# Splitting the transposed rows ahead of the evacuation, and the product g behind both, in a fused convolution and feed-forward kernel on one core

## The chip, the cores and the metric

The kernel runs on one NeuronCore of a Trainium2 chip. The core has five engines that matter here: TensorE (PE, with its weight loads shown apart as PEld), VectorE (DVE), ScalarE (ACT), GpSimd (POOL) and SyncE (SP, which issues the DMAs). Each engine works through its own queue in order; engines wait for each other through semaphores. The metric is the device time of one execution in microseconds, as the median of several runs. Lower is better.

## What is computed

The first stage is a convolution along the sequence whose seven taps differ for every position and head: the taps are a softmax of `weight_gen`. The second stage is a feed-forward layer with the activation h cos h. Sizes: 8 x 4096 tokens, 192 channels, 8 heads of 24 channels, 7 taps, 2048 hidden columns; x and the taps arrive in float32, the two weight matrices in float64.

```python
w = exp(weight_gen - max(weight_gen, axis=-1))
w = w / (sum(w, axis=-1) + 1e-9)                      # [B, S, H, 7]
x_pad = concatenate([zeros(B, 6, D), x], axis=1)
x_unf = x_pad[:, arange(S)[:, None] + arange(7)[None, :], :].reshape(B, S, 7, H, 24)
y = einsum('bshk,bskhg->bshg', w, x_unf).reshape(B * S, D)
h = y @ w_in                                          # [32768, 2048]
g = h * cos(h)
out = (g @ w_out).astype(float32)                     # [32768, 192]
```

## The kernel before

**Tiling.** Each of the 128 partitions holds a run of 256 consecutive tokens. A block is four tokens of every partition (R = 4), so 512 tokens; there are 64 blocks (NB). The 2048 hidden columns are taken in pairs of chunks of 128, eight pairs a block (NPAIR). One period of the main loop (L537) is one pair of one block; there are 512 periods (N) and a tail of six (LAG). Products are made accurate by splitting an operand into a high part, rounded for PE, and a low rest, with three products in place of one: x_hi and x_lo for the mixed rows, ghi and glo for g, wa_hi, wa_lo, wb_hi and wb_lo for `w_in`.

**Mixing.** `attention` (L213) computes the seven products and six sums of a block on POOL. `attentions` (L457) is a generator, and every period takes some steps of it (L585), so that this work lies between the other work of POOL. A block's mixing may start when the block two before it is transposed (L459), because its buffer `xa` exists twice. `until_mixed` (L468) puts the remaining steps into the queue at once.

**Transposing.** PE needs the mixed rows with channels on partitions. For the first blocks (up to WHOLE) `transpose_all` (L276) transposes a whole block into a PSUM tile of the kind that also holds h, in pair 5 of the block before. Later blocks are transposed row by row: `transpose_row` (L285) puts a row's transposed channels into columns 384 to 511 of the accumulator tile `acc`, whose columns 0 to 383 hold sums of the output. `split` (L268) then reads the transposed rows twice: ACT writes x_hi (L270), DVE writes x_lo (L272), which needs x_hi. The x_hi and x_lo tiles exist twice, by turns for even and odd blocks.

**The feed-forward period.** For period i, PE computes h of pair i in two portions: `ffn_in_first` (L318, matmuls L326) before and `ffn_in_second` (L332, matmuls L343) after `ffn_out` (L380), which multiplies g of six periods ago (j = i - 6) with `w_out` into `acc` (L400). The elementwise work on h of pair i - 1 is a chain between ACT and DVE: turn (L353, ACT: h plus a quarter, rounded to an integer), fraction (L357, DVE), cos (L361, ACT) and g (L364, DVE). For pair i - 2, ACT makes ghi (hi, L370) and DVE glo (lo, L374). h has three PSUM tiles; the one that pair i takes is free when lo of pair i - 3 is done.

**The accumulator.** `acc` (L387) is one PSUM tile of two banks, and there is only one (the pool at L79). Two periods fill it, an even j and an odd j: a group. After the odd one, `evacuate` (L412) reads it: ACT copies the sums into a `part` tile (L421; here called the evacuation), then `split` reads the transposed rows. The first matmul of the next group can only overwrite `acc` when these reads are over. POOL adds the parts (L437, L438), and SP stores four rows of a block at a time (L443), three periods later.

**What sets the order.** The order in which the text issues instructions is the order in each engine's queue; the last loop (L590) nails it down with a dependency between neighbours. In a period the text issues: turn of i - 1, hi of i - 2, fraction and cos of i - 1, lo of i - 2, g of i - 1 (L539 to L552), then PE's matmuls (L561 to L568), then the evacuation and the split (L576), then a step of the softmax (L584), then mixing steps. Which row of which block lies in which accumulator is fixed in `ffn_out` (L406) and again in `evacuate` (L422):

```python
bt = group // R + 2
if WHOLE < bt < NB:
    transpose_row(bt, group % R, acc, s)
```

The softmax of the next sixteen rows is started in every fourth block and runs one step a period (L580 to L584); its exponential (L183) is ACT's, and needs another function table than the cosine.

Of the kernel before, what the change touches and what calls it, by code (L numbers as in the profile page):

```python
# [11 lines left out]
F32 = mybir.dt.float32  # L12
# [8 lines left out]
P = 128  # L21
# [20 lines left out]
def tile_softmax_conv_then_cos_ffn(  # L42
# [17 lines left out]
    R = 4  # L60
# [7 lines left out]
    HALF = NPAIR // 2  # L68
    LAG = 6
    TR = 5  # L70
    WHOLE = 6
    TMP = 6
    CW = 512

    const = ctx.enter_context(tc.tile_pool(name="const", bufs=1))
# [209 lines left out]
    def transpose_row(b, r, acc, s):  # L285

        xa = mixed[b]
        for q in range(2):
            rs = slice(q * D2, (q + 1) * D2)
            nc.tensor.matmul(acc[:, q ^ s, 2 * D + q * D2:2 * D + (q + 1) * D2],  # L290
                             lhsT=xa[rs, r, columns(q ^ s)], rhs=ident[rs, rs], is_transpose=True,
                             start=False, stop=True, skip_group_check=True)
        if r == R - 1 and s == 1:
            transposed.add(b)
# [23 lines left out]
    def ffn_in_first(i):  # L318

        b, pair = divmod(i, NPAIR)  # L320
        x_hi, x_lo = xT[b]
        h = ps_h.tile([P, 2, CT], F32, name="h")
        for m, (w, v) in enumerate(((wa_hi, x_lo), (wa_lo, x_hi), (wa_hi, x_hi))):
            for q in range(2):
                rs = slice(q * D2, (q + 1) * D2)
                nc.tensor.matmul(  # L326
                    h[:, q, :], lhsT=w[rs, chunk(pair, q)], rhs=v[rs, 0, :],
                    start=(m == 0), stop=False, skip_group_check=True)
        hs[i] = h
        traded(h)  # L330
# [49 lines left out]
    def ffn_out(j):  # L380

        b, m = divmod(j, 2 * R)
        half, m = divmod(m, R)
        tp, s = divmod(m, 2)
        group = j // 2
        if s == 0:
            accs[group] = ps_m.tile([P, 2, CT], F32, name="acc")  # L387
        acc = accs[group]
        whole = j + LAG >= N
        for lo in range(2):  # L390
            for c in range(2 * HALF):
                pair, n = divmod(c, 2)
                g = g_parts[b * NPAIR + half * HALF + pair][lo]
                fc = half * 2 * HALF + c
                for q in range(1 if whole else 2):
                    rs = slice(0, P) if whole else slice(q * D2, (q + 1) * D2)
                    bank = q ^ s
                    t = 2 * tp + bank
                    to, w = (acc[:, bank, 0:2 * D], wo) if lo == 0 else (acc[:, bank, 0:D], wo_b)
                    nc.tensor.matmul(  # L400
                        to, lhsT=g[rs, n, t * P:(t + 1) * P], rhs=w[rs, fc, :],
                        start=(lo == 0 and c == 0 and (whole or s == 0)),
                        stop=(lo == 1 and c == 2 * HALF - 1 and (whole or s == 1)),
                        skip_group_check=True)
            if lo == 0:
                bt = group // R + 2  # L406
                if WHOLE < bt < NB:
                    transpose_row(bt, group % R, acc, s)
        if s == 0 and not whole:
            traded(acc)  # L410

    def evacuate(j):  # L412
        b, m = divmod(j, 2 * R)
        half, m = divmod(m, R)
        tp, s = divmod(m, 2)
        if s == 0:
            return
        group = j // 2
        acc = accs.pop(group)
        part = work.tile([P, 2, 2 * D], F32, name=f"part{half}", bufs=2)  # L420
        nc.scalar.activation(out=part, in_=acc[:, :, 0:2 * D], func=AF.Copy, scale=TWO_PI)  # L421
        bt = group // R + 2  # L422
        if WHOLE < bt < NB:
            r = group % R
            yield from split(bt, acc[:, :, 2 * D:], slice(r * P, (r + 1) * P))
        if half == 0:
            sums[(b, tp)] = part
            return
        if tp == 0:
            fin_t = work.tile([P, R, D], F32, name="fin")  # L430
            finals[b] = fin_t
        fin = finals[b]
        old = sums.pop((b, tp))
        last = b == NB - 1
        eng = nc.vector if last else nc.gpsimd
        ts = slice(2 * tp, 2 * tp + 2)
        eng.tensor_tensor(out=part, in0=part, in1=old, op=ALU.add)  # L437
        eng.tensor_tensor(out=fin[:, ts, :], in0=part[:, :, 0:D], in1=part[:, :, D:2 * D],  # L438
                          op=ALU.add)
        if tp == 1 or last:  # L440
            t0 = 2 * tp if last else 0
            def store(t0=t0):
                nc.sync.dma_start(out=o_v[:, :, (b * R + t0) * D:(b * R + 2 * tp + 2) * D],  # L443
                                  in_=fin[:, t0:2 * tp + 2, :].rearrange("p r d -> p (r d)"))

            if last:
                store()
            else:
                stores[j + LATE] = store
        if tp == 1:  # L450
            finals.pop(b)
            for pair in range(NPAIR):
                g_parts.pop(b * NPAIR + pair)
# [83 lines left out]
    for i in range(N + LAG + 1):  # L537

        if 0 <= i - 1 < N:  # L539
            act_turns(i - 1)  # L540
        if 0 <= i - 2 < N:
            act_hi(i - 2)
        for c in converts.get(i - 1, ()):
            next(c)
        if 0 <= i - 1 < N:
            dve_fraction(i - 1)
            act_cos(i - 1)
        all_of(*converts.pop(i - 1, ()))
        if 0 <= i - 2 < N:
            dve_lo(i - 2)  # L550
        if 0 <= i - 1 < N:
            dve_g(i - 1)  # L552
        if i == N + LAG:
            break
        b, pair = divmod(i, NPAIR)
        j = i - LAG
        if b < NB and pair == 0:
            assert b in transposed
        if 0 <= j and j % (2 * R) == 0 and WHOLE < j // (2 * R) + 2 < NB:
            until_mixed(j // (2 * R) + 2)  # L560
        if j < 0:  # L561
            ffn_in_whole(i)
        else:
            if i < N:
                ffn_in_first(i)
            ffn_out(j)
            if i < N:
                ffn_in_second(i)  # L568
        tr = ()
        if pair == TR and b + 1 <= WHOLE:  # L570
            until_mixed(b + 1)
            tr = (transpose_all(b + 1),)
        if j in stores:
            stores.pop(j)()
        if j >= 0:
            all_of(evacuate(j), *tr)  # L576
        else:
            all_of(*tr)
        load_weights(i + AHEAD)
        if b % SB == SB - 1 and pair == SMP and b + 4 < NB:  # L580
            r0 = (b + 4) * R
            sm = softmax(r0, min(r0 + RW, RPP), nc.gpsimd)
        if i >= NPAIR + SMP:
            next(sm, None)  # L584
        for _ in range(4 if i == 0 else 2 + i % 2 if i < 60 else 2):  # L585
            next(bg, None)


# [39 lines left out]
```

## Time and profile before

| | us |
|---|---|
| median of 3 runs | 2451.38 |
| lowest and highest of these | 2450.24 and 2451.68 |
| the profiled execution's own time | 2449.39 |
| its span, first to last instruction | 2447.6 |

| engine | busy us | of the span |
|---|---|---|
| PE | 2278.4 | 93% |
| DVE | 2034.2 | 83% |
| POOL | 1848.4 | 76% |
| ACT | 1833.8 | 75% |

The granted PE clock has a mean of 0.985 over the span. The page lists groups of instructions by source line, with the number of instructions, their busy time, the mean duration in nanoseconds and the idle time of their engine just before them. Each of the six instructions of the elementwise chain runs 512 times: turn 1024 ns, hi 1012 and cos 1060 on ACT; fraction 1222, g 1232 and lo 1214 on DVE. The evacuation runs 256 times with 794 ns. The timeline gives single instructions with start and duration in microseconds, merged where neighbours are alike ("x16"), and, in brackets, the idle time of the engine before them and what ended it. An instruction on DVE or ACT may show its start a little before its predecessor's end, since the engines pipeline.

### The profile page before, as it was taken

Reading aid. Unit: us, or ns where it says so; the run is one execution under the profiler, and the core shown is the slowest. Engines: PE = TensorE matmul, PEld = TensorE weight load, DVE = VectorE, ACT = ScalarE, POOL = GpSimd, SP = SyncE. Lnnn points to the kernel's source line nnn. Section 1 sums busy time; section 2 is a strip of 40 time slices with the busy share of each in tenths; the row PEclk is TensorE's granted clock in tenths of the full one; section 3 lists DMA queues with packets and bytes.
Section 4 is the critical chain, followed back from the end, with each engine's and each line's share of the span. In section 5 each row is a group of like instructions: output and inputs, shape, how many; then the busy total and the mean of one; then the engine's idle time right before and its main releaser. Section 6 shows DMA issues by size and latency. Waiting matters only on the chain.

```text
span 2447.6 us, 60709 instructions
## 1 busy us (share of the span) xinstructions
PE 2278.4 (93%) x26436; PEld 1951.2 (80%) x26436; DVE 2034.2 (83%) x1923; ACT 1833.8 (75%) x2117; POOL 1848.4 (76%) x1206
## 2 busy tenths in 40 slices
PE   2799999999999999999999999999999999999998
PEld 1577887878788788888878788788888878788887
DVE  8878788888888888888888888888888888888886
ACT  3667777777777777777777777777777777777776
POOL 7589777878878878777878878878777778878730
PEclk8799999999999999999999999999999999999999
DMA  5112111111112112111111112112111111211100
GB/s 145 36 40 54 43 35 47 46 32 47 48 31 54 41 29 54 46 32 47 47 31 46 48 31 54 43 28 54 43 35 47 47 32 47 49 29 48 25 14 21
DMA packets 25689, 105.56 MB, mean 43 GB/s; under 512 B 2654, under 2 KB 6486, under 8 KB 25422
## 3 DMA queue, kind: packets, MB, share of 16 engines
q1 hardware_dynamic: 25422, 101.67, 16.9%
q8 instruction: 207, 3.39, 0.6%
q14 instruction: 60, 0.49, 0.1%
HBM read 76.50 MB, written 25.17 MB: 42 GB/s over the span
## 4 chain that ended last, share of the span: by engine, by line
PE 53%; DVE 25%; ACT 12%; issue 9%; DMA 1%; ACTq 0%; SPq 0%; DVEq 0%
PE acc L400 30%; PE h L343 19%; DVE turn L357 9%; DVE glo L374 8%; ACT turn L353 7%; DVE x_lo L272 4%; PE h L326 4%; DVE h L364 1%; ACT x_hi L270 1%; ACT L183 1%; ACT turn L361 1%; ACT ghi L370 1%; PE acc L290 1%; DVE den L187 1%; DMA taps<-in_weight_gen_dram 1%
## 5 line engine op out<-in xcount | busy, mean ns | idle before, releaser
L357 DVE TENSOR_TENSOR turn<-h,turn 128x1024 f32<-128x1024 f32 x512 | 625.7, 1222 | 365.6 <-ACT turn L353 365.5
L400 PE MATMUL acc<-wo,ghi 64*128 64x384 f32 x8144 | 838.5, 343 | 50.1 <-DVE x_lo L272 47.2
L400 PEld LDWEIGHTS acc<-wo,ghi 64*128 64x128 f32 x8144 | 723.6, 187 | 173.4 <-DVE x_lo L272 145.9
L353 ACT ACTIVATE turn<-h 128x1024 int32<-128x1024 f32 x512 | 524.4, 1024 | 298.6 <-PE h L343 296.1
L244 POOL TENSOR_TENSOR xa<-xa,pr 128x768 f32<-128x768 f32 (+1 forms) x384 | 705.4, 1837 | 5.0
L361 ACT ACTIVATE turn<-turn 128x1024 f32<-128x1024 f32 x512 | 542.8, 1060 | 221.5 <-DVE turn L357 221.2
L364 DVE TENSOR_TENSOR h<-h,turn 128x1024 f32<-128x1024 f32 x512 | 631.0, 1232 | 13.8 <-ACT turn L361 13.8
L374 DVE TENSOR_TENSOR glo<-h,ghi 128x1024 bf16<-128x1024 f32 x512 | 621.8, 1214 | 1.1 <-ACT ghi L370 1.1
L224 POOL TENSOR_TENSOR pr<-xt,taps 128x768 f32<-128x768 f32 (+1 forms) x384 | 586.9, 1536 | 18.3
L437 POOL TENSOR_TENSOR part<-part,part 128x768 f32<-128x768 f32 x126 | 232.2, 1843 | 483.4 <-ACT part L421 483.3
L370 ACT CAST ghi<-h 128x1024 fp32r<-128x1024 f32 x512 | 518.0, 1012 | 8.4 <-DVE h L364 8.2
L400 PE MATMUL acc<-wo_b,glo 64*128 64x192 bf16 x8144 | 424.3, 243 | 0.0
L400 PEld LDWEIGHTS <-glo 64*128 64x128 bf16 x8144 | 331.4, 94 | 25.4 <-issue 7.8
L326 PE MATMUL h<-x_lo,wa_hi 64*128 64x512 f32 x1012 | 206.4, 402 | 56.9 <-DVE glo L374 42.6
L343 PE MATMUL h<-x_lo,wa_hi 64*128 64x512 f32 x1012 | 241.9, 473 | 0.0
L421 ACT ACTIVATE part<-acc 128x768 f32<-128x768 f32 x256 | 203.3, 794 | 9.2 <-PE acc L400 9.2
L343 PE MATMUL h<-x_lo,wb_hi 64*128 64x512 f32 x1012 | 202.4, 395 | 0.0
L326 PE MATMUL h<-x_hi,wa_hi 64*128 64x512 f32 x1012 | 201.6, 393 | 0.0
L343 PE MATMUL h<-x_hi,wa_hi 64*128 64x512 f32 x1012 | 201.1, 392 | 0.0
L326 PE MATMUL h<-x_hi,wa_lo 64*128 64x512 f32 x1012 | 200.7, 391 | 0.0
L343 PE MATMUL h<-x_hi,wb_hi 64*128 64x512 f32 x1012 | 200.1, 390 | 0.0
L343 PE MATMUL h<-x_hi,wb_lo 64*128 64x512 f32 x1012 | 199.5, 389 | 0.0
(74 smaller groups left out, 2047.7 us busy)
## 6 DMA issues: line engine op xcount, KB each, us to landing
xt<-in_x_dram SPq DMA_DIRECT2D x62, 960.0 KB, 6.8
out_dram<-fin SPq DMA_DIRECT2D x63, 384.0 KB, 3.4
taps<-in_weight_gen_dram SPq DMA_DIRECT2D x15, 448.0 KB, 4.3
raw<-in_moe_w_out_dram SPq DMA_DIRECT2D x8, 384.0 KB, 5.3
raw<-in_moe_w_in_dram SPq DMA_DIRECT2D x6, 256.0 KB, 6.1
raw<-in_moe_w_in_dram SPq DMA_DIRECT2D x3, 512.0 KB, 12.2
xt<-in_x_dram SPq DMA_DIRECT2D x1, 768.0 KB, 12.0
xt<-in_x_dram SPq DMA_DIRECT2D x1, 540.0 KB, 6.7
```

The lines of the kernel that those rows point to most:

```text
L224: eng.tensor_tensor(out=dst.rearrange("p r (h g) -> p r h g", h=H), in0=xt[:, k + ra:k + rb, :].rearrange("p r (h g) -> p r h g", h=H), in ...
L244: eng.tensor_tensor(out=xa[:, ra:rb, 0:D], in0=xa[:, ra:rb, 0:D], in1=old[:, ra:rb], op=ALU.add)
L326: nc.tensor.matmul(h[:, q, :], lhsT=w[rs, chunk(pair, q)], rhs=v[rs, 0, :], start=(m == 0), stop=False, skip_group_check=True)
L343: nc.tensor.matmul(h[:, 1 - q, :], lhsT=w[rs, cs], rhs=v[rs, part, :], start=False, stop=(m == len(prods) - 1), skip_group_check=True)
L353: nc.scalar.activation(out=t.bitcast(I32), in_=hs[i], func=AF.Identity, bias=0.25, scale=1.0)
L357: nc.vector.tensor_tensor(out=t, in0=hs[i], in1=t.bitcast(I32), op=ALU.subtract)
L361: nc.scalar.activation(out=t, in_=t, func=AF.Sin, bias=SIN_BIAS, scale=SIN_SCALE)
L364: nc.vector.tensor_tensor(out=hs[i], in0=hs[i], in1=turns.pop(i), op=ALU.mult)
L370: nc.scalar.copy(out=hi, in_=hs[i])
L374: nc.vector.tensor_tensor(out=lo, in0=hs.pop(i), in1=hi.bitcast(F32), op=ALU.subtract)
L400: nc.tensor.matmul(to, lhsT=g[rs, n, t * P:(t + 1) * P], rhs=w[rs, fc, :], start=(lo == 0 and c == 0 and (whole or s == 0)), stop=(lo == 1 ...
L437: eng.tensor_tensor(out=part, in0=part, in1=old, op=ALU.add)
```

## The change

Four things change together.

- In `evacuate` the split comes before the evacuation: ACT's queue has x_hi and then the copy into `part`; x_lo follows x_hi on DVE. In the main loop g of i - 1 is issued behind the evacuation and the split, not ahead of PE's matmuls; the split of a whole block (`tr`) comes behind g.
- The rows of a block are transposed one group, that is two periods, later: row r of block bt lies in group 4 bt + r - 7, before in 4 bt + r - 8. The last row is then split in the last period before the block's first. `until_mixed` moves along. In `ffn_in_first` the product with x_lo comes last, before it came first.
- WHOLE is 5, before 6: block 6 is transposed by rows.
- TMP, the number of `turn` buffers, is 5, before 6; `part0` has three buffers, before two; fewer mixing steps are issued in the first 48 periods (three in every fourth period and two in the others, before two and three by turns).

```diff
@@ -68,8 +68,8 @@
-    WHOLE = 6
-    TMP = 6
+    WHOLE = 5
+    TMP = 5
@@ -320,7 +320,7 @@
-        for m, (w, v) in enumerate(((wa_hi, x_lo), (wa_lo, x_hi), (wa_hi, x_hi))):
+        for m, (w, v) in enumerate(((wa_lo, x_hi), (wa_hi, x_hi), (wa_hi, x_lo))):
@@ -403,9 +403,9 @@
             if lo == 0:
-                bt = group // R + 2
+                bt, r = divmod(group + 2 * R - 1, R)
                 if WHOLE < bt < NB:
-                    transpose_row(bt, group % R, acc, s)
+                    transpose_row(bt, r, acc, s)
@@ -417,12 +417,11 @@
         acc = accs.pop(group)
-        part = work.tile([P, 2, 2 * D], F32, name=f"part{half}", bufs=2)
+        bt, r = divmod(group + 2 * R - 1, R)
+        if WHOLE < bt < NB:
+            yield from split(bt, acc[:, :, 2 * D:], slice(r * P, (r + 1) * P))
+        part = work.tile([P, 2, 2 * D], F32, name=f"part{half}", bufs=(3 if half == 0 else 2))
         nc.scalar.activation(out=part, in_=acc[:, :, 0:2 * D], func=AF.Copy, scale=TWO_PI)
-        bt = group // R + 2
-        if WHOLE < bt < NB:
-            r = group % R
-            yield from split(bt, acc[:, :, 2 * D:], slice(r * P, (r + 1) * P))
@@ -548,16 +547,15 @@
-        if 0 <= i - 1 < N:
-            dve_g(i - 1)
...
-        if 0 <= j and j % (2 * R) == 0 and WHOLE < j // (2 * R) + 2 < NB:
-            until_mixed(j // (2 * R) + 2)
+        bt, r = divmod(j // 2 + 2 * R - 1, R)
+        if 0 <= j and j % 2 == 0 and r == 0 and WHOLE < bt < NB:
+            until_mixed(bt)
@@ -573,16 +571,17 @@
         if j >= 0:
-            all_of(evacuate(j), *tr)
-        else:
-            all_of(*tr)
+            all_of(evacuate(j))
+        if 0 <= i - 1 < N:
+            dve_g(i - 1)
+        all_of(*tr)
...
-        for _ in range(4 if i == 0 else 2 + i % 2 if i < 60 else 2):
+        for _ in range(4 if i == 0 else 3 if i < 48 and i % 4 == 0 else 2):
             next(bg, None)
```

## The prediction

> **What bounds the kernel now.** I read the page's busy shares and its chain first, then the list of waits, then the timeline of one steady stretch, row by row.
>
> ```profile
> PE 2278.4 (93%) x26436; PEld 1951.2 (80%) x26436; DVE 2034.2 (83%) x1923; ACT 1833.8 (75%) x2117; POOL 1848.4 (76%) x1206
> ...
> PE 53%; DVE 25%; ACT 12%; issue 9%; DMA 1%; ACTq 0%; SPq 0%; DVEq 0%
> ```
>
> ```profile
> POOL part L437 <- ACT part L421: 483.3, 122, 23.9
> ...
> PEld acc L400 <- DVE x_lo L272: 145.9, 228, 0.9
> ```
>
> PE is the busiest engine, yet DVE and ACT hold 37% of the chain, so PE does not run free. Where it stops is plain: 228 times, once for each group whose accumulator also carries transposed rows, the first weight load of the next group waits for x_lo (L272). POOL has 483 us of waiting for the evacuation and is not on the path.
>
> The timeline of two periods (the first evacuates, the second does not), engine by engine; columns are start, duration, engine, line:
>
> ```profile
> 1202.95 1.03 ACT L353 ACTIVATE turn<-h 128x1024 int32<-128x1024 f32 x1 [1.30 <-PE h L343]
> 1203.87 1.01 ACT L370 CAST ghi<-h 128x1024 fp32r<-128x1024 f32 x1
> 1205.27 1.06 ACT L361 ACTIVATE turn<-turn 128x1024 f32<-128x1024 f32 x1 [0.39 <-DVE turn L357]
> 1206.23 0.80 ACT L421 ACTIVATE part<-acc 128x768 f32<-128x768 f32 x1
> 1206.92 0.37 ACT L270 ACTIVATE x_hi<-acc 128x256 fp32r<-128x256 f32 x1
> 1207.19 1.02 ACT L353 ACTIVATE turn<-h 128x1024 int32<-128x1024 f32 x1
> ...
> 1204.01 1.22 DVE L357 TENSOR_TENSOR turn<-h,turn 128x1024 f32<-128x1024 f32 x1 [1.09 <-ACT turn L353]
> 1205.15 1.21 DVE L374 TENSOR_TENSOR glo<-h,ghi 128x1024 bf16<-128x1024 f32 x1
> 1206.36 1.23 DVE L364 TENSOR_TENSOR h<-h,turn 128x1024 f32<-128x1024 f32 x1
> 1207.50 0.41 DVE L272 SCALAR_TENSOR_TENSOR x_lo<-acc,x_hi 128x256 fp32r<-128x256 f32 x1
> ...
> 1202.93 0.19 PEld L326 LDWEIGHTS h<-x_hi,wa_hi 64*128 64x128 f32 x2
> 1203.16 1.47 PEld L400 LDWEIGHTS acc<-wo,ghi 64*128 64x128 f32 x16
> ...
> 1207.17 0.19 PEld L326 LDWEIGHTS h<-x_hi,wa_hi 64*128 64x128 f32 x2
> 1207.97 1.35 PEld L400 LDWEIGHTS acc<-wo,ghi 64*128 64x128 f32 x16 [0.61 <-DVE x_lo L272]
> ...
> 1211.40 0.19 PEld L326 LDWEIGHTS h<-x_lo,wa_hi 64*128 64x128 f32 x2
> ...
> 1202.47 0.39 PE L343 MATMUL h<-x_hi,wb_hi 64*128 64x512 f32 x2
> 1202.70 0.39 PE L326 MATMUL h<-x_lo,wa_hi 64*128 64x512 f32 x2
> ...
> 1206.94 0.40 PE L326 MATMUL h<-x_lo,wa_hi 64*128 64x512 f32 x2
> ...
> 1211.62 0.40 PE L326 MATMUL h<-x_lo,wa_hi 64*128 64x512 f32 x2
> ```
>
> Count from the fraction on DVE (L357, 1204.01), called F. The chain is: F, lo (L374) at F+1.14, g (L364) at F+2.35, x_lo at F+3.49, done at F+3.90, weight load at F+3.96 (a hop of 0.06 from DVE to PE). Unhindered, that load follows the last one of L326 by 0.23, as 1203.16 follows 1202.93; here this would be 1207.40 (1207.17 + 0.23), F+3.39. So the wait costs 0.57 us at the load. The pair takes 8.92 us (1202.70 to 1211.62). It is a closed loop: the load releases L400, then L343, then turn (L353), then the next F. PE work outside this loop, in the evacuating period, has half a microsecond to spare.
>
> What the pace would be without the wait is shown by the stretch in which rows are transposed by whole blocks, and block 5 stands beside block 6 there:
>
> ```profile
> 267.18 1.03 ACT L353 ACTIVATE turn<-h 128x1024 int32<-128x1024 f32 x1 [0.83 <-PE h L343]
> ...
> 275.61 1.03 ACT L353 ACTIVATE turn<-h 128x1024 int32<-128x1024 f32 x1 [0.83 <-PE h L343]
> ...
> 305.15 1.03 ACT L353 ACTIVATE turn<-h 128x1024 int32<-128x1024 f32 x1 [1.15 <-PE h L343]
> ...
> 340.92 1.03 ACT L353 ACTIVATE turn<-h 128x1024 int32<-128x1024 f32 x1 [1.15 <-PE h L343]
> ```
>
> 267.18 to 275.61 is 8.43 us for two periods; with row transposes it would be twice 4.24 (1202.70 to 1206.94, the unhindered starts of L326), 8.48. So 0.44 us per pair, 228 times, is the prize: some 100 us. Block 5 (267.18 to 305.15) takes 37.97 us, block 6 35.77.
>
> **The change part by part.** *Split ahead of the evacuation, g behind both.* On DVE x_lo no longer stands behind g; on ACT x_hi takes the place of the evacuation. But x_hi, x_lo and the evacuation all read acc, a tile of the same two banks, and PE is released by the last. In the rows above no two engines read acc at once: ACT ends at 1207.29 (1206.92 + 0.37), DVE begins at 1207.50. I take it that the program keeps this so in the new order too; then the evacuation, now last in the text, waits for x_lo. The chain becomes: cos at F+1.26; x_hi at F+2.22 (the place of L421 now), done F+2.60 (0.38); x_lo 0.03 to 0.04 later (below), F+2.63 to F+3.04; the evacuation after a hop from DVE to ACT of 0.03 (1204.01 + 1.23 = 1205.24 to 1205.27), F+3.07, done 0.80 later at F+3.87; load 0.06 later at F+3.93, the hop taken from DVE's row since ACT's is not among these.
>
> The Trainium skill, "PSUM — Partial Sum Buffer", section Terms, says that ScalarE and VectorE on one bank and quadrant at the same time are a collision error, "reads against reads included". The trace agrees so far as it has no such pair.
>
> The hop may be longer. An ACT instruction with one wait starts 0.05 after PE's last matmul, one with several 0.09 (1202.86 to 1202.95 above):
>
> ```profile
> 1215.63 0.39 PE L343 MATMUL h<-x_hi,wb_hi 64*128 64x512 f32 x2
> ...
> 1216.07 0.39 ACT L270 ACTIVATE x_hi<-acc 128x256 fp32r<-128x256 f32 x1
> ...
> 1216.49 0.42 DVE L272 SCALAR_TENSOR_TENSOR x_lo<-acc,x_hi 128x256 fp32r<-128x256 f32 x1
> ```
>
> The evacuation waits for its part buffer as well in three groups of four (each buffer is freed by POOL's L437 or L438; the third part0 only makes one of the waits needless), so I add 0.04 there: load at F+3.97, against F+3.96 now. Per pair, -0.03 to +0.01; over a block about nothing. **The stall of 0.57 us stays and changes its owner**, from x_lo to the evacuation. Bounds: -0.03 x 228 = -7 us, and +11 if the hop costs 0.05 more.
>
> Queued behind the waiting evacuation on ACT is turn of the other period: it starts 0.69 after it (1206.92 - 1206.23), at F+3.80, now F+3.18. That moves its F to F+4.86, lo to F+6.00, ending F+7.21; the weight load at 1211.40 (F+7.39) needs lo: 0.1 us to spare, and as that PE work lies outside the loop, a small overrun is absorbed. g is late to F+2.97, done F+4.20; hi of the next period (L370, 0.92 after turn) comes at F+4.72. Nothing else waits.
>
> *Rows two pairs later.* The first row of a block now writes x_hi (two buffers) when the block before last is done with it. Today that x_hi waits for L343 of its own period (1216.02 to 1216.07), which makes the fourth pair about 0.07 longer. Of 57 row blocks (6 to 62), 43 are without the softmax below: -3 us. In exchange the last row is split in the period just before its block starts; x_hi is there at F+2.66, x_lo at F+3.10, while L326 loads at F+2.69 and, x_lo's product now being third, F+3.16 (1207.17). If that fails, PE is late for a place where it waits until F+3.97 anyway: nothing. Mixing on POOL, its xt load on SP and its deadline move together, by two periods; POOL's 483 us cover it.
>
> *Five whole blocks.* Block 5 becomes a row block, 37.97 to 35.77: -2.2 us. One more pair with rows at the end: 8.92 for 8.43, +0.5.
>
> *Softmax in the row stretch.* 14 times (every fourth block from 7 to 59, L580) ACT loads the exponential's table at the end of an evacuating period:
>
> ```profile
> 506.20 1.22 DVE L357 TENSOR_TENSOR turn<-h,turn 128x1024 f32<-128x1024 f32 x1 [0.52 <-ACT turn L353]
> ...
> 509.12 0.38 ACT L270 ACTIVATE x_hi<-acc 128x256 fp32r<-128x256 f32 x1
> 509.51 1.28 ACT L183 ACT_TABLE_LOAD   x1
> 510.81 0.95 ACT L183 ACTIVATE taps<-taps 128x896 f32<-128x896 f32 x1
> 511.66 1.01 ACT L353 ACTIVATE turn<-h 128x1024 int32<-128x1024 f32 x1
> ...
> 515.11 0.50 PE L326 MATMUL h<-x_lo,wa_hi 64*128 64x512 f32 x2 [1.13 <-DVE glo L374]
> ```
>
> Here ACT's queue is the path: load, exp, turn, then lo on DVE, and PE waits 1.13 for lo. Now the load follows x_hi (509.50); then it follows the evacuation, 506.20 + 3.87 to 3.91 = 510.07 to 510.11. The whole tail is 0.6 us later: +8.5 us over 14. Nothing covers it. PE's idle there grows, and the clock can drop:
>
> ```profile
> 515.00:530.00 15.00, 13.00 (x134) 11.25 (x136) 11.58 (x13) 9.64 (x11) 13.36 (x9) 0.89 0.39 94
> ```
>
> A granted clock of 0.89 over 15 us is 1.7 us lost. I allow one drop more, +2 (0 to +6). By the Trainium skill, "TensorE: Matmul & The Clock Gate", section What's actually happening, the clock drops after an idle window of about 3.4 us; the stretch with 0.89 holds the wait of 1.13 us quoted above and PE is busy for 13.00 of its 15 us, so trace and page differ. By the page the sum would be 2 us less.
>
> *Start.* TMP 5 for 6 holds one turn and two conversions with two to spare. Two mixing steps fewer on POOL by period 8, while conversions on DVE are sometimes stretched:
>
> ```profile
> 63.73 0.43 DVE L117 TENSOR_SCALAR t<-t 128x512 f32<-128x512 f32 x1 [0.44 <-ACT t L115]
> ...
> 79.81 1.75 DVE L117 TENSOR_SCALAR t<-t 128x512 f32<-128x512 f32 x1 [0.44 <-ACT t L115]
> ```
>
> The same instruction took 0.43 and 1.75 us. Two such stretches fewer would be -2.6, three more +4; I take -2.
>
> **Sum:** 0 - 3 - 2.2 + 0.5 + 8.5 + 2 - 2 = +3.8 us. On the profiled execution (2449.39, span 2447.6) that is 2453.2, on the median of three runs (2451.38, which is 2.0 above it) 2455.2. I give 2454.
>
> **The rivals.** *ACT reads beside DVE* (5%): if the evacuation does not wait for x_lo, it starts 0.27 behind x_hi (1207.19 - 1206.92), at F+2.49, and is done at F+3.29, the load free at F+3.35 before F+3.39. Then 57 row blocks lose 4 x 0.44 us, block 5 4 us, and 2449 - 100 - 4 = 2345. For it: the two read different columns. Against it: the rows and the page named above.
>
> *Shorter hops and a lighter start* (18%): -0.03 in every pair (-7), start -5, no drop of the clock: 2449.4 - 7 - 3 - 2.2 + 0.5 + 8.5 - 5 = 2441, or 2443 by the median.
>
> *The evacuation's wait costs more than a hop* (20%), the one that ends slower. Its place is ACT's queue between x_lo and L421. The evacuation is inside the loop, so each 0.1 us there costs 23 us over 228 pairs. It decides from 0.08 us on, where the load passes F+3.98. At 0.12 it is +9 on top: 2463.
>
> That the change does not do what it says is not a case: the order of the text is the order of the queues.
>
> **How the numbers follow.** The forecast (57%) has its own range of 2446 to 2460. A difference under 0.2% (4.9 us, so 2446.5 to 2456.3) cannot be told from none. Of its 57, 42 are within, 13 slower, 2 faster; the rivals give 5 and 18 faster, 20 slower: faster 0.25, same 0.42, slower 0.33. The range goes from 2439 to 2466; outside stay the 5% of 2345, some 4% below and 10% above.
>
> **What would show it.** Right: L400's weight load waits for ACT's L421, about 0.6 us, some 230 times, and no longer for x_lo; x_hi at F+2.2, x_lo at F+2.6, the evacuation at F+3.1; a plain row block near 35.7 us; the table load 0.6 later after its F; block 5 near 35.8. Wrong: an evacuation that starts before x_lo has ended, L400 with no wait, a block near 33.9, or a wait for lo at L326 in plain blocks.

## The result, and the profile after

| | before | after |
|---|---|---|
| median, us | 2450.73 (6 runs, 2448.64 to 2451.68) | 2463.32 (6 runs, 2459.54 to 2469.20) |
| ratio to before, 95% interval | | 1.0054 (1.0039 to 1.0070) |
| profiled execution, us | 2449.39 | 2466.11 |
| its span, us | 2447.6 | 2464.3 |

The changed kernel is slower by 0.54%, some 12.6 us. The forecast was 2454, no change that can be measured, with a chance of 0.33 for slower; the time lies inside the range (2439 to 2466), near its upper end. It also agrees with the time of the rival that ends slower, 2463, but as will be seen in the main for another reason. The six executions of the changed kernel fall into two groups, 2459.5 to 2460.5 and 2466.1 to 2469.2 us, and the profiled one belongs to the second, so that its span shows a larger loss (16.7 us) than the medians do; what parts the groups is not shown.

The page of the changed kernel, its busy shares and its chain:

```profile
PE 2286.2 (93%) x26444; PEld 1956.9 (79%) x26444; DVE 2037.8 (83%) x1926; ACT 1854.4 (75%) x2120; POOL 1844.3 (75%) x1206
...
PE 42%; ACT 24%; DVE 20%; issue 13%; ACTq 0%; DMA 0%; SPq 0%; DVEq 0%
```

The shares of busy time have hardly moved, but ACT's share of the chain has doubled from 12% to 24%. The list of waits (us in total, times, longest) says where:

```profile
PEld acc L400 <- ACT part L424: 150.9, 235, 2.3
ACT part L424 <- DVE x_lo L272: 121.6, 229, 0.8
...
POOL taps L192 <- DVE den L190: 43.0, 15, 3.7
```

The first weight load of a group waited 228 times for x_lo, 145.9 us in all; now it waits 235 times for the evacuation (L424 in this kernel), 150.9 us, and the evacuation waits for x_lo. This is the change of owner that was forecast. The timeline of an evacuating period of the changed kernel (start, duration, engine, line):

```profile
1203.26 1.22 DVE L357 TENSOR_TENSOR turn<-h,turn 128x1024 f32<-128x1024 f32 x1 [0.48 <-ACT turn L353]
...
1205.48 0.36 ACT L270 ACTIVATE x_hi<-acc 128x256 fp32r<-128x256 f32 x1
...
1205.88 0.43 DVE L272 SCALAR_TENSOR_TENSOR x_lo<-acc,x_hi 128x256 fp32r<-128x256 f32 x1 [0.26 <-ACT x_hi L270]
...
1206.40 0.81 ACT L424 ACTIVATE part<-acc 128x768 f32<-128x768 f32 x1 [0.55 <-DVE x_lo L272]
...
1207.26 1.35 PEld L400 LDWEIGHTS acc<-wo,ghi 64*128 64x128 f32 x16 [0.64 <-ACT part L424]
```

Counted from the fraction at 1203.26 (F): x_hi F+2.22, x_lo F+2.62, evacuation F+3.14, load F+4.00. The three reads of acc still stand one behind the other, and their sum is nearly what it was: the load was at F+3.96.

So where do 16.7 us of span come from? The starts of turn (L353) of every eighth period cut the span into blocks:

| stretch | before, us | after, us | difference |
|---|---|---|---|
| to the first turn of block 5 | 267.18 | 267.98 | +0.8 |
| block 5 | 37.97 | 35.82 | -2.2 |
| 43 blocks with rows, without softmax | 1537.4 (median 35.76) | 1538.5 (median 35.79) | +1.1 |
| 14 blocks with a softmax | 553.3 (39.07 to 40.83) | 570.2 (38.33 to 42.07) | +16.9 |
| the rest | 51.7 | 51.8 | +0.1 |

All of it is in the 14 softmax blocks. Their new times fall into classes: 39.65 us four times, about 40.45 three times, 41.84 to 42.07 six times, and the last one 38.33 (it gained 2.1). One of the 40.45 (from 931.94 on) shows a thing that the prediction had not looked at:

```profile
962.51 1.08 DVE L187 TENSOR_REDUCE den<-taps 128x128 f32<-128x896 f32 x1
...
963.02 1.55 POOL L224 TENSOR_TENSOR xa<-xt,taps 128x768 f32<-128x768 f32 x1 [0.29 <-PE acc L290]
963.62 1.03 DVE L188 TENSOR_SCALAR den<-den 128x128 f32<-128x128 f32 x1
964.53 1.54 POOL L224 TENSOR_TENSOR pr<-xt,taps 128x768 f32<-128x768 f32 x1
964.58 1.21 DVE L357 TENSOR_TENSOR turn<-h,turn 128x1024 f32<-128x1024 f32 x1
965.82 1.06 ACT L361 ACTIVATE turn<-turn 128x1024 f32<-128x1024 f32 x1 [2.18 <-DVE turn L357]
966.78 0.37 ACT L270 ACTIVATE x_hi<-acc 128x256 fp32r<-128x256 f32 x1
...
967.20 0.19 PEld L326 LDWEIGHTS h<-x_hi,wa_lo 64*128 64x128 f32 x2 [2.62 <-ACT x_hi L270]
```

L188 adds 1e-9 to 128 denominators of every partition. It takes 1.03 us and ends at 964.65, 0.08 after POOL's product (963.02 + 1.55 = 964.57). Behind it on DVE stands the fraction, behind that on ACT cos and x_hi, and for x_hi, the last row of the next block, PE waits 2.62 us. In the four blocks of 39.65 us POOL had no instruction under way when the addition began, and it took 0.23 us; in the other nine full softmax blocks it took 1.02 to 1.04. One view, the durations of L188 (min/median/max in ns), for before and then after:

```profile
L188 DVE TENSOR_SCALAR den<-den x18: 181/386/1590, 5.0 to 2278.5; 128x128 f32<-128x128 f32 x15, 128x32 f32<-128x32 f32 x2, 128x64 f32<-128x64 f32 x1
```

```profile
L188 DVE TENSOR_SCALAR den<-den x18: 181/1027/1320, 5.0 to 2297.4; 128x128 f32<-128x128 f32 x15, 128x32 f32<-128x32 f32 x2, 128x64 f32<-128x64 f32 x1
```

The theory that went into the experiments: the plain blocks are as forecast; of the loss, one part is the table load that stands 0.6 us later on ACT, as forecast, and the other part is this addition. POOL's L224 writes the buffer xa, so it waits for the transposition of the last row (L290), and since rows are transposed two periods later it now runs beside the addition. Where PE then waits long enough, its clock drops, which adds 1.6 us (about 42.05 beside 40.45).

### The profile page after: what moved, and what is told of

Read it like the earlier page. It is cut to its first block, busy times and chain, and to the rows that moved or that the text cites. A ratio compares the mean times of both kernels' runs of the same rounds, so it can differ in the third digit from the quotient of the medians.

```text
span 2464.3 us, 60868 instructions
## 1 busy us (share of the span) xinstructions
PE 2286.2 (93%) x26444; PEld 1956.9 (79%) x26444; DVE 2037.8 (83%) x1926; ACT 1854.4 (75%) x2120; POOL 1844.3 (75%) x1206
## 3 DMA queue, kind: packets, MB, share of 16 engines
q8 instruction: 208, 3.41, 0.6%
## 4 chain that ended last, share of the span: by engine, by line
PE 42%; ACT 24%; DVE 20%; issue 13%; ACTq 0%; DMA 0%; SPq 0%; DVEq 0%
PE acc L400 25%; PE h L343 15%; DVE turn L357 12%; ACT turn L353 10%; ACT part L424 7%; DVE x_lo L272 4%; ACT x_hi L270 4%; PE h L326 1%; DVE h L364 1%; ACT turn L361 1%; ACT L183 1%; ACT ghi L370 1%; DVE den L187 1%; ACT taps L183 1%; PE acc L290 1%
## 5 line engine op out<-in xcount | busy, mean ns | idle before, releaser
L400 PEld LDWEIGHTS acc<-wo,ghi 64*128 64x128 f32 x8144 | 724.2, 187 | 174.5 <-ACT part L424 150.9
L353 ACT ACTIVATE turn<-h 128x1024 int32<-128x1024 f32 x512 | 523.9, 1023 | 183.5 <-PE h L343 181.8
L224 POOL TENSOR_TENSOR pr<-xt,taps 128x768 f32<-128x768 f32 (+1 forms) x384 | 587.7, 1536 | 13.8
L400 PE MATMUL acc<-wo_b,glo 64*128 64x192 bf16 x8144 | 429.4, 245 | 0.0
L424 ACT ACTIVATE part<-acc 128x768 f32<-128x768 f32 x256 | 207.4, 810 | 132.4 <-DVE x_lo L272 121.6
L326 PE MATMUL h<-x_hi,wa_lo 64*128 64x512 f32 x1012 | 205.1, 401 | 66.0 <-DVE glo L374 33.9
L343 PE MATMUL h<-x_lo,wa_hi 64*128 64x512 f32 x1012 | 243.4, 477 | 0.0
L343 PE MATMUL h<-x_lo,wb_hi 64*128 64x512 f32 x1012 | 202.2, 395 | 0.0
L326 PE MATMUL h<-x_hi,wa_hi 64*128 64x512 f32 x1012 | 200.5, 392 | 0.0
L326 PE MATMUL h<-x_lo,wa_hi 64*128 64x512 f32 x1012 | 200.4, 391 | 0.0
L343 PE MATMUL h<-x_hi,wa_hi 64*128 64x512 f32 x1012 | 200.4, 392 | 0.0
L343 PE MATMUL h<-x_hi,wb_hi 64*128 64x512 f32 x1012 | 199.8, 390 | 0.0
L343 PE MATMUL h<-x_hi,wb_lo 64*128 64x512 f32 x1012 | 199.4, 389 | 0.0
```

The costliest lines, as they stand in the source:

```text
L224: eng.tensor_tensor(out=dst.rearrange("p r (h g) -> p r h g", h=H), in0=xt[:, k + ra:k + rb, :].rearrange("p r (h g) -> p r h g", h=H), in ...
L326: nc.tensor.matmul(h[:, q, :], lhsT=w[rs, chunk(pair, q)], rhs=v[rs, 0, :], start=(m == 0), stop=False, skip_group_check=True)
L343: nc.tensor.matmul(h[:, 1 - q, :], lhsT=w[rs, cs], rhs=v[rs, part, :], start=False, stop=(m == len(prods) - 1), skip_group_check=True)
L353: nc.scalar.activation(out=t.bitcast(I32), in_=hs[i], func=AF.Identity, bias=0.25, scale=1.0)
L400: nc.tensor.matmul(to, lhsT=g[rs, n, t * P:(t + 1) * P], rhs=w[rs, fc, :], start=(lo == 0 and c == 0 and (whole or s == 0)), stop=(lo == 1 ...
```

## The experiments

All comparisons with the kernel before were made on the same chip as the run itself. Where a run is compared with the changed kernel's 2463.32 us, the two are from different sessions; the medians of the kernel before lie between 2449.63 and 2450.73 us in all of them. Sums over blocks are of one profiled execution each.

**One: the copy first.** ACT copies the sums and then makes x_hi; the rest stays as changed.

```diff
+        part = work.tile([P, 2, 2 * D], F32, name=f"part{half}", bufs=(3 if half == 0 else 2))
+        nc.scalar.activation(out=part, in_=acc[:, :, 0:2 * D], func=AF.Copy, scale=TWO_PI)
         bt, r = divmod(group + 2 * R - 1, R)
         if WHOLE < bt < NB:
             yield from split(bt, acc[:, :, 2 * D:], slice(r * P, (r + 1) * P))
-        part = work.tile([P, 2, 2 * D], F32, name=f"part{half}", bufs=(3 if half == 0 else 2))
-        nc.scalar.activation(out=part, in_=acc[:, :, 0:2 * D], func=AF.Copy, scale=TWO_PI)
```

> The changed kernel with one thing undone: ACT copies the sums first and makes x_hi behind it; g stays behind both on DVE. Theory (acc is released by the last of three reads that stand one behind the other, and the new order only put the longest of them last): the copy starts at F+2.22, x_hi 0.70 later at F+2.92, x_lo at F+3.32, the weight load at F+3.79 in place of F+4.00, so about 0.2 us less in each of some 230 pairs, a plain row block near 35.0 in place of 35.75; in the softmax blocks the table load comes 0.6 us earlier, some 8 us over 14. Together near 2410 us. Rival (the order of the three reads is worth nothing, and what was lost lies elsewhere): 2463 us, plain blocks at 35.75.

Measured: 2455.16 us, 1.0022 of before (1.0013 to 1.0030). A miss of 45 us, with the mechanism in place:

```profile
1024.25 1.22 DVE L357 TENSOR_TENSOR turn<-h,turn 128x1024 f32<-128x1024 f32 x1 [0.41 <-ACT turn L353]
...
1027.57 0.42 DVE L272 SCALAR_TENSOR_TENSOR x_lo<-acc,x_hi 128x256 fp32r<-128x256 f32 x1 [0.97 <-ACT x_hi L270]
...
1028.05 1.35 PEld L400 LDWEIGHTS acc<-wo,ghi 64*128 64x128 f32 x16 [0.45 <-DVE x_lo L272]
...
1036.37 0.19 PEld L326 LDWEIGHTS h<-x_hi,wa_lo 64*128 64x128 f32 x2 [0.68 <-ACT x_hi L270]
```

The load is at F+3.80 (1028.05 - 1024.25), and a pair takes 8.77 us for 8.96: 0.2 each, as expected. But the last pair of a block takes 9.01, since PE comes to the next block at 1036.37 and the last row's x_hi, now behind the copy, is not there. A plain block is 35.31, not 35.0. And the softmax blocks became longer, 580.7 us in the sum for 570.2: the addition was held in all 13 of the 128-wide ones (1.01 to 1.04), and the clock dropped in 12.

**Two: without the addition.** The line L188 runs for the first softmax only.

```diff
-        nc.vector.tensor_scalar_add(out=den, in0=den, scalar1=1e-9)
+        if r0 == 0:
+            nc.vector.tensor_scalar_add(out=den, in0=den, scalar1=1e-9)
```

> The changed kernel without the addition of 1e-9 to the softmax's denominators (L188), for all softmaxes behind the first; the output lacks that term. Theory (in 9 of the 14 softmax blocks this small DVE instruction is held for 0.8 us by POOL's product L224, which now starts beside it): those 9 blocks come down by 0.8 us or somewhat more, 40.45 to about 39.6; the whole by about 7 us, to 2456 us, give or take 4 for clock drops that fall differently. Rival (the instruction waits where DVE has time; the loss is the table load on ACT and the clock): 14 times its normal 0.23, at most 3 us, 2460 us or above.

Measured: 2443.11 us, 0.9973 of before (0.9962 to 0.9984), 20 us below the changed kernel. All 13 full softmax blocks take 39.38 to 39.42, the last 38.16, and no clock drop is left among them. The instruction of 0.23 us was worth 1.4 us a block (19.9 over 14), nearly three times what the theory gave, because the drops that cost time went with it. (The largest of the seven exponentials is exp(0) = 1, and float32 numbers near 1 are 6e-8 or more apart, so adding 1e-9 does not change a sum of them.)

**Three: rows at their old time.** All else as changed.

```diff
-                bt, r = divmod(group + 2 * R - 1, R)
+                bt, r = divmod(group + 2 * R, R)
```

(the same in `evacuate`, and for `until_mixed` in the main loop)

> The changed kernel with its rows transposed two periods earlier again, as before; all else stays. Theory (the later rows brought POOL's L224 beside the addition L188): the addition takes 0.4 us or less in all 14 softmax blocks, so 7 us less there; the first row of a block waits again for L343, 0.07 us in 43 blocks, 3 us more; near 2459 us, with runs spread as little as those of the kernel before. Rival (the long additions come from the order on ACT, which makes the exponential end 0.6 us later): the additions stay long, and the time is 2463 to 2467 us.

Measured: 2500.74 us, 1.0206 of before (1.0192 to 1.0220). The part on the addition came true: 0.65 us in 13 of 13, softmax blocks at 40.1 with a clock drop in 2. The part on the first row was wrong by a factor of 13:

```profile
1049.19 0.41 PE L343 MATMUL h<-x_hi,wb_hi 64*128 64x512 f32 x2
...
1049.63 0.38 ACT L270 ACTIVATE x_hi<-acc 128x256 fp32r<-128x256 f32 x1 [0.81 <-PE h L343]
...
1051.37 1.18 PEld L400 LDWEIGHTS acc<-wo,ghi 64*128 64x128 f32 x14 [1.51 <-ACT part L424]
```

x_hi of the first row may be written only after L343 of its own period, which reads the same buffer for another block. Before, x_hi stood behind the evacuation and waited 0.05. Now it stands at the head of the chain, waits 0.81, and the load behind it 1.51: this pair takes 9.83 us (5.77 + 4.06) for 8.91, a plain block 36.72 for 35.79. Transposing the rows later is what makes the split bearable at the head of the chain; without that part the split would cost 0.9 us more in every block.

**Four: the softmax a period later.**

```diff
-    SMP = 2
+    SMP = 3
```

> The changed kernel with its softmax begun one period later (SMP 3 in place of 2), so that the exponential falls into a period without an evacuation. Theory (ACT's queue is the path in the 14 softmax blocks, and the exponential's table load now stands behind the copy): table load and exponential, 2.2 us, meet a period in which ACT has about 1.2 us less to do; a softmax block goes from 40.7 in the mean to between 37.5 and 39.7, the whole to between 2420 and 2449 us. Rival (a softmax block costs what its own instructions take, wherever they stand): 2460 us or above.

Measured: 2461.10 us, 1.0042 of before (1.0030 to 1.0055): the rival was right. In the block from 1076.97 on the period with the exponential falls from 7.18 to 5.33 us, and the next one grows from 4.19 to 5.99. ACT's queue is caught up a period later, and the addition, one period later too, meets another of POOL's instructions:

```profile
964.69 1.83 POOL L244 TENSOR_TENSOR xa<-xa,pr 128x768 f32<-128x768 f32 x1
...
965.68 0.93 DVE L188 TENSOR_SCALAR den<-den 128x128 f32<-128x128 f32 x1
```

It is held in all 13 (0.92 to 0.97), and 10 clock drops are left.

**Five: the kernel before without the addition.** The edit of run two, in the kernel before.

> The kernel before, without the addition of 1e-9 behind the first softmax; a sum of exponentials that holds exp(0) = 1 does not change in float32 when 1e-9 is added. Theory (POOL's hold on that small DVE instruction is the only difference in the softmax blocks beside the table load that the change put behind the copy): the addition took 0.38 here, so an undisturbed softmax block goes from 39.09 to about 38.8, the four with a clock drop from 40.4 to 40.8 to the same, and the whole to 2440 us, give or take 3. Measured against the changed kernel without the addition (2443), the change then still costs 13 times 0.6 in the softmax blocks less 2.2 for block 5. Rival (the addition is free where it isn't held, and the drops come from elsewhere): 2449 us or above, drops as before.

Measured: 2436.99 us, 0.9950 of before (0.9938 to 0.9963). Softmax blocks go to 38.66, a little below the 38.8 expected, and one clock drop is left of four. With run two this gives the change without the addition on both sides: the medians differ by 6.1 us, the sums of the 14 softmax blocks by 8.4 (550.3 and 541.9). This is 0.6 us a block in the mean, the price that the prediction gave to the table load behind the copy. But run five's sum holds a drop of 1.6 us; blocks without one differ by 0.73 (39.39 and 38.66). In the pair that holds the exponential 0.66 of it is seen directly: 6.52 + 4.19 before, 7.18 + 4.19 after.

**Six and seven: the copy first without the addition, with rows late and early.** Run six is run one without the addition. Run seven is the kernel before, without the addition, with only g moved:

```diff
-        if 0 <= i - 1 < N:
-            dve_g(i - 1)
         if i == N + LAG:
             break
...
         if j >= 0:
-            all_of(evacuate(j), *tr)
-        else:
-            all_of(*tr)
+            all_of(evacuate(j))
+        if 0 <= i - 1 < N:
+            dve_g(i - 1)
+        all_of(*tr)
```

> The changed kernel with the copy of the sums first, and without the addition of 1e-9. Theory (the copy-first order gained 0.45 us in every plain block, and lost it in the softmax blocks, where the addition was held in all 13 and the clock dropped in 12): the softmax blocks go from between 41.5 and 42.8 to about 39.0, no drop is left, and the whole is 2420 us, give or take 4. Rival (softmax blocks of this order are long because the copy-first order makes x_lo late, whatever the addition does): 2440 us or above, with drops left.

> The kernel before with one part of the change alone: g behind the evacuation and the split, so ACT copies, then makes x_hi, and x_lo follows at once; rows at their old time, block 6 transposed whole; and without the addition of 1e-9. Theory (x_lo need not be late for the next block when rows are transposed two periods earlier, which made the last pair of e1's blocks 9.01 in place of 8.77; and since x_hi stands behind the copy its wait for L343 costs the 0.07 it cost before): four pairs of 8.77 and 0.07, a plain block near 35.15, softmax blocks near 38.4, the whole near 2408 us. Rival (early rows cost 0.9 us a block with the g-behind order, as in the run with rows early): plain blocks at 36.0, 2455 us.

Measured: 2428.63 us, 0.9914 of before (0.9901 to 0.9928), and 2421.16 us, 0.9885 (0.9872 to 0.9899). Run six lies between its theory and its rival: blocks without a drop are at 38.92, as expected, but 8 drops of the clock remain, 1.6 us each. So the addition isn't the only thing that leads to them. Run seven refutes its rival (35.30, not 36.0), but is 13 us above its theory: the first row's wait for L343 costs 0.23 here (that pair takes 9.00 for 8.77), not 0.07, and a full softmax block takes 38.79 for 38.4. It has no drop in its softmax blocks. Rows early or late are worth the same in a plain block when the copy comes first (35.30 and 35.29): early, the first row waits, late, the last row is waited for.

**Eight and nine: rows from a copy.** Nothing that reads acc waits for another engine: ACT copies the transposed columns out, then the sums; x_hi and x_lo are made from the copy, x_lo on POOL. The rest is the kernel before with WHOLE 5; run eight leaves the addition out, run nine has it.

```diff
+        if rows_too:
+            r = group % R
+            xr = work.tile([P, 2, P], F32, name="xr", bufs=2)
+            nc.scalar.activation(out=xr, in_=acc[:, :, 2 * D:], func=AF.Copy, scale=1.0 / TWO_PI)
         part = work.tile([P, 2, 2 * D], F32, name=f"part{half}", bufs=2)
         nc.scalar.activation(out=part, in_=acc[:, :, 0:2 * D], func=AF.Copy, scale=TWO_PI)
+        if rows_too:
+            hi, lo = parts_of(bt)
+            cs = slice(r * P, (r + 1) * P)
+            nc.scalar.copy(out=hi[:, :, cs], in_=xr)
+            nc.gpsimd.tensor_tensor(out=lo[:, :, cs], in0=xr, in1=hi[:, :, cs].bitcast(F32), op=ALU.subtract)
```

> The order of the kernel before, in which ACT copies the transposed columns out of acc first (0.37 us, new tile xr), then the sums; x_hi comes from xr on ACT, x_lo from xr on POOL, so that no read of acc waits for another engine; WHOLE 5; without the addition of 1e-9. Theory (PE is held by nothing in the plain blocks but acc's release): acc is free at F+2.22 + 0.27 + 0.81 + 0.06 = F+3.36, ahead of the F+3.39 at which PE comes to it; a pair takes 8.43 to 8.5, a plain block 33.9, a softmax block 36.9 to 37.8; the whole is 2335 to 2355 us. Rival 1 (ACT, with 0.37 more to do in each pair, or POOL's x_lo coming late, becomes the bound): plain blocks at 34.8 or above, 2395 us or above. Rival 2 (another limit of about 4.4 a period stands behind the stall): plain blocks at 35.2, 2415 us.

> The run with the rows taken from a copy, with the addition of 1e-9 put back into every softmax; nothing else differs. It parts the gain of that run into acc's release and the addition. Theory (the release is worth 57 times 1.8 us, the addition 10 to 20 us as far as POOL holds it): plain blocks stay at 33.97, only softmax blocks change, by 0.4 us each if the addition takes 0.4, by up to 2.5 with the drops of the clock that follow if it is held for 1.0; 2345 to 2372 us. Rival (with x_lo off DVE the addition finds another place and is not held, or PE no longer waits for the softmax): 2340 us, as without it.

Measured: 2340.10 us, 0.9551 of before (0.9538 to 0.9564), and with the addition 2359.58 us, 0.9631 (0.9617 to 0.9645). The timeline of a steady pair of run eight:

```profile
967.36 1.22 DVE L357 TENSOR_TENSOR turn<-h,turn 128x1024 f32<-128x1024 f32 x1 [0.31 <-ACT turn L353]
...
969.58 0.36 ACT L425 ACTIVATE xr<-acc 128x256 f32<-128x256 f32 x1
...
969.84 0.81 ACT L427 ACTIVATE part<-acc 128x768 f32<-128x768 f32 x1
...
970.55 0.21 PEld L326 LDWEIGHTS h<-x_hi,wa_hi 64*128 64x128 f32 x2
970.80 1.48 PEld L400 LDWEIGHTS acc<-wo,ghi 64*128 64x128 f32 x16
...
971.36 0.75 POOL L432 TENSOR_TENSOR x_lo<-xr,x_hi 128x256 fp32r<-128x256 f32 x1
```

The copy ends at 970.65 (F+3.29), and the load at 970.80 shows no wait: it follows the load of L326 before it by 0.25. A pair takes 8.49 us, a plain block 33.97, where 33.9 was expected. The page's chain is now PE's:

```profile
PE 86%; DVE 6%; ACT 5%; issue 2%; DMA 0%; SPq 0%; POOL 0%; ACTq 0%; DVEq 0%
```

Of the gain of 110 us over before, 91 come with acc's earlier release (run nine; some 4 of them are block 5, now with rows, at 33.98 for 37.97), and 19 with leaving out the addition, which in run nine is held longest of all (1.32 to 1.36 in 13 of 13). The same edit takes x_lo, 0.41 us a pair, off DVE; no run parts that from the release, though the load's wait for acc, which is gone, speaks for the release. Run eight is the fastest of the study; among the kernels that keep the addition it is run nine.

**Ten: POOL out of the addition's way.** The changed kernel, complete; only the first two mixing products of the next block stand behind the softmax's product L192 in POOL's queue.

```diff
-        for _ in range(4 if i == 0 else 3 if i < 48 and i % 4 == 0 else 2):
+        held = lambda i: i > 48 and i // NPAIR % SB == SB - 1 and i % NPAIR == NPAIR - 1
+        for _ in range(4 if i == 0 else 3 if i < 48 and i % 4 == 0 else 0 if held(i) else 4 if held(i - 1) else 2):
```

> The changed kernel, complete, with the addition of 1e-9; only POOL's queue differs: in the 13 softmax blocks of the row stretch the first two mixing products of the next block (L224) stand behind the softmax's product L192, where before they stood ahead of it, so that POOL has nothing to do while DVE adds. Theory (POOL's work holds the addition): it takes 0.23 in all softmax blocks, no clock drop that costs time is left, a softmax block takes 39.4 plus at most 0.3, and the whole is 2444 to 2449 us. Rival (something else makes the addition long, or the drops come without it): additions of 1.0 in some nine blocks, 2460 us or above.

Measured: 2452.82 us, 1.0012 of before (1.0003 to 1.0021), 10.5 us below the changed kernel's median. The same place in the same block as above, now without POOL:

```profile
959.77 1.07 DVE L187 TENSOR_REDUCE den<-taps 128x128 f32<-128x896 f32 x1
...
960.88 0.23 DVE L188 TENSOR_SCALAR den<-den 128x128 f32<-128x128 f32 x1
961.02 1.22 DVE L357 TENSOR_TENSOR turn<-h,turn 128x1024 f32<-128x1024 f32 x1
...
963.65 0.18 PEld L326 LDWEIGHTS h<-x_hi,wa_lo 64*128 64x128 f32 x2 [1.82 <-ACT x_hi L270]
```

0.23 us in 13 of 13, PE's wait 1.82 for 2.62, softmax blocks at 39.67, and one at 41.26 with a drop that costs time. That is the theory, by the addition and the blocks. The median is 4 us above its range: in the profiled run 1.3 us are in the start, 228.0 us for the first 40 periods against 226.7 in the changed kernel, and 1.6 in the one drop.

## Why the prediction was right, and where it was not

**What bounds the kernel: right.** The three reads of acc in a row hold PE, and moving the longest to the end changes the owner and not the sum. Run one shows the chain from one side (0.2 us a pair by the order of the reads), runs eight and nine from the other: with no read waiting for another engine the pair is 8.49, where the prediction read 8.48 off the unhindered starts. Its first rival put 2345 on an acc released early; run nine, which releases it in another way, gives 2360.

**Pairs, 0 (bounds -7 to +11), and the first row, -3: the first a little low, the second right.** x_hi and x_lo start within 0.01 of the forecast. The evacuation's hop is 0.09 us (1205.88 + 0.43 to 1206.40) in 146 of 232 groups, those in which the evacuation waits for a second thing beside x_lo, and 0.03 in the other 86; the forecast was 0.07 and 0.03. So the load shown comes at F+4.00, not at F+3.97. Three pairs of a block are 0.03 to 0.04 longer, and the fourth, without the wait for L343, is 0.08 shorter (8.91 for 8.99). Over the 42 plain blocks ahead of period 496 that is +4.2 and -3.7 us. The rival that made the hop dear named 0.08 us as the hop from which it counts, and this was reached: it holds in part, by an estimate from these 42 blocks at some 6 us over 57, two thirds of its 9.

**Block 5, -2.2, and the end, +0.5: right.** 37.97 to 35.82 is -2.15, and the block from period 496 on goes from 35.13 to 35.76, +0.6.

**The table load on ACT, +8.5: right.** Runs two and five part it from the rest: +8.4 in the sums, and 0.73 in place of 0.6 us in a block without a drop.

**The clock, +2 (0 to +6), and POOL's mixing, put at nothing: this is the step that failed.** What stands in its place is +8.5 us: 19.9 us that the addition, with the drops behind it, costs in the softmax blocks of the changed kernel (570.2 - 550.3), less 11.4 in those of the kernel before (553.3 - 541.9). The prediction went through the softmax block by ACT's queue alone, and gave DVE's small instruction and POOL no sentence. It had the evidence in its own rows: the same kind of instruction at L117 once at 0.43 and once at 1.75 us, quoted there for the start and not followed to L188. Runs three and ten show that it is POOL's neighbourhood: 0.65 us with the old rows, 0.23 with POOL idle. Which part of the 8.5 is the instruction itself and which the clock isn't parted cleanly; a held addition with no drop is 0.8 us a block (40.45 and 39.65), one with a drop that costs time is 2.4.

**Rows two pairs later: right in the changed kernel, but undervalued.** It was priced as it stood in the old order, -3 us; run three shows that in the new one it saves 37. The sentence that it moves POOL's mixing by two periods, covered by 483 us of POOL's waiting, priced POOL's own queue only and not whom POOL meets.

**The start, -2 (-6 to +4): not to be told.** The first 40 periods took 226.1 us before and 226.7 after; over the seven traces with the changed start they lie between 223.4 and 228.0. The smaller parts of the change (TMP, the third part0, the mixing steps, the order of the three products) were not run by themselves.

**The sum.** +3.8 us was forecast; 12.6 were measured in the medians and 16.7 in the profiled executions. The time lies in the range because the range was wide on the slow side, for a dear hop and for clock drops; that an addition on DVE would fill it was luck.

**The expectation of run one** was wrong for the same reason as the prediction: it took the softmax blocks to gain from the earlier exponential, and took no account of the new block's first reader of x_hi.

## What to carry to other kernels

When several engines read one accumulator in turn, the release is the sum of the reads and hops, and reordering them moves it little (here by 0.04 to 0.2 us of 4.0); take the dependence between engines out of the chain, as a short copy by the engine that reads anyway did here (0.36 us on ACT bought 0.43 us a pair). When a step is moved in time, ask not only whether its engine has room but which instructions of other engines it will now run beside. And count a rare event by its whole path: 14 softmax blocks carried all of the loss.

## What the runs showed of the hardware

**A DVE addition of 0.23 us is held by POOL.** With POOL idle it took 0.23 us in 13 of 13 cases (run ten); beside POOL's products and sums 0.38 to 1.36. Over all traces 93 additions, those of narrower tiles among them, began while a POOL instruction was under way; 92 ended 0.03 to 0.09 us after it, and in the other one POOL had only 0.07 us left. The reduction (L187) of the same tile took 1.07 to 1.08 us in every run, though in six of the traces it began beside a running POOL instruction 13 times of 15. The reciprocal (L190) took 0.94 to 0.95; it met a running POOL instruction only once or twice in a trace. By the Trainium skill, "SBUF — State Buffer", section SBUF: two separate sides, DVE and GpSimd share a pair of ports that is locked for a whole instruction, by DVE only in certain modes or with two operands in SBUF; the traces agree, in that the addition ends when POOL's instruction has ended, 0.08 us after it in the rows above. In which mode the addition ran, no trace shows.

**The clock is set window by window.** The granted clock falls only on a grid of 3.413 us, and to half. The view by stretches, on that grid, for the changed kernel (length; then busy time and instructions of PE, PEld, DVE, ACT and POOL; granted clock; DMA share; GB/s):

```profile
963.22:966.63 3.41, 1.80 (x22) 1.18 (x16) 3.38 (x4) 1.23 (x2) 2.85 (x2) 1.00 0.00 0
966.63:970.04 3.41, 2.50 (x24) 1.99 (x26) 3.15 (x5) 2.92 (x5) 0.30 (x1) 1.00 0.00 0
1113.38:1116.80 3.42, 1.50 (x12) 1.02 (x14) 3.15 (x5) 2.72 (x4) 0.46 (x1) 1.00 0.00 0
1116.80:1120.21 3.41, 3.41 (x34) 3.28 (x32) 3.41 (x4) 2.30 (x3) 2.70 (x2) 0.50 0.02 5
```

After a window with PE busy 1.80 of 3.41 us (53%) the next runs at full clock; after one with 1.50 of 3.42 (44%) at half. Over the twelve traces, from 290 to 2300 us, a drop began behind 29 of 30 windows under 45%, 36 of 63 from 45 to 53%, 1 of 21 up to 57.5%, and none of 6953 above. Four drops, all in run one, lasted two windows. Whether a wait of PE brings a drop depends on how it falls on the grid: the emptiest stretch of 3.41 us has PE busy 46 to 47% in each of run six's 13 full softmax blocks, and 8 of them have a drop. In run two it is 48 to 49%, and none has; in run ten the same, and two have. Run seven's softmax blocks are nearly as long as run six's, but their emptiest stretch is 61 to 62% busy, and none has a drop. The Trainium skill, "TensorE: Matmul & The Clock Gate", section What's actually happening, gives a free-running window of 3413 ns, and the traces agree; it names an idle window as the condition, and here a window half idle was enough. A drop where PE waits for others anyway costs nothing, as in the changed kernel's four blocks of 39.65 us, which all have one, beside 39.67 without one in run ten.
